# One inverse transform for all four heads: the full-height inverse of heads 0 and 1 replaced by the packed half-height one

## The chip, the cores and the metric

One core of one Trainium2 chip. The time is the device time of one execution in microseconds (us); where several executions are compared, it is the median. TensorE (PE, with its weight loads PEld), VectorE (DVE), ScalarE (ACT), GpSimd (POOL) and the DMA queue of SyncE (SP) work side by side, each strictly in its own order.

## The reference: what is computed

Two independent heads, concatenated along the last axis. Sequence 2048, width 512, float32.

```
A (FNet):  a = x @ Wd_re.T ; b = x @ Wd_im.T            # DFT over the width
           ya = Ws_re @ a - Ws_im @ b                    # DFT over the sequence, real part
B (S4D):   A = -exp(log_A_real) + 1j*A_imag ; dt = exp(log_dt)
           K[d,l] = 2*Re( sum_n C[d,n]*dt[d] * exp(A[d,n]*dt[d]*l) )      # 512 x 2048, 128 states
           y  = irfft( rfft(u, 4096) * rfft(K, 4096) )[:2048]            # causal convolution
           yb = y + u * D_skip
out = concat([ya, yb], -1)
```

## The kernel before, in words

**FNet** (class `Fnet`) is matmul work: 1920 matmuls of 128x128 by 128x512 (L312, tile `acc`). Each float32 operand is split into a rounded `hi` and a remainder `lo` (type fp32r), and three products hi*hi, hi*lo, lo*hi replace one. `split` (L147) does it: ScalarE copies `raw` into `hi` (L150), VectorE subtracts to get `lo` (L155). The first operand of all is `items[groups[0]][0]`, a tile `sT`; TensorE's first FNet matmul needs its `hi`. Some tiles take another way: GpSimd's DMA rounds and accumulates them (L248, L253). FNet has no deadline of its own: its matmuls fill TensorE between the steps of the other part.

**S4D** (class `Ssm`) runs as a chain of steps on four quarters of the width, h = 0 to 3 (`PART` = 128 columns each):

- VectorE builds exponential tables in 16 chunks (`tables1`, `tables2`; L531 to L648, tiles `t1`, `t2`, `prod`, `cs`, with seeds from ScalarE). For each chunk TensorE runs one `taps` block (L735), which needs both tables of the chunk. After every second chunk comes one block of `stage1_k` (L779): its result goes to DRAM as `xk`.
- u passes through `stage1_u` (L840): ScalarE and VectorE evacuate it (L851, L853, L855), it goes to DRAM as `xu`.
- For each quarter and q = 0 to 3, `product` loads `xu` and `xk`, runs the second stage of the forward transform (L975), multiplies on VectorE (L962 to L1000), and pairs of q go through the first stage of the inverse transform (`first_inverses`, L1009). The result is stored to DRAM as `zs` (L1047).
- The second stage of the inverse transform is run twice for each quarter (i = 0, 1). It loads `zs` transposed into a tile `zl`, does one TensorE block, is evacuated by ScalarE and stored to `out_yb`. There are two forms of it. `inverse` (L1122 on, quarters 0 and 1) uses the table `ib` with the whole height of 128 rows and two 128x64 tiles of the array side by side. `inverse2` (quarters 2 and 3, `HALVED` = 2) first adds and subtracts the two halves of the spectrum on VectorE (L1089, L1091), and then needs half of the rows: eight 64x32 tiles of the array side by side, with the table `ib2`. `ib2` is loaded over `ib` once all four calls of `inverse` are done (`load_ib2`).

**The order** of every engine's instructions is written out by hand: each coroutine yields the engine it wants next (`"pe"`, `"act"`, `"dve"`, `"dma"`, `"pool"`), and `Plan.run` steps them in the order of the list `ORDER`, some 2,700 numbers. `TURNS` is the order in which coroutines take the two PSUM tiles `f0` and `f1`. Buffers are counted with semaphores (`Sem`): `zls` for the tiles `zl`, `zbs` for the tiles `z` (`ZS` gives their number: 2 in the first set of buffers, 4 in the second).

The matmuls of the two forms, the old one and then the packed one:

```
for w in range(n // 2):            # inverse: 16 matmuls, K = 128, 64 columns
    for y in range(2):
        nc.tensor.matmul(ps[64 * y:64 * y + 64, ...], self.ib[:, n * i + 2 * w + y], z[:, 2 * w + y], ...,
                         tile_position=(0, 64 * y))
for o in range(0, c, 2):           # inverse2: 32 matmuls, K = 64, 32 columns
    for x in range(4):
        for y in range(2):
            nc.tensor.matmul(ps[32 * x:32 * x + 32, y, ...], self.ib2[r, c * i + w, x % 2], (t, z[:, 1])[x % 2][r, w], ...,
                             tile_position=(64 * y, 32 * x))
```

Of the kernel before, what the change touches and what calls it, by code (L numbers as in the profile page):

```python
# [26 lines left out]
def fft_constants():  # L27
# [24 lines left out]
    return [np.ascontiguousarray(a.astype(np.float32)) for a in (f1u, f1k, w2, ia, ib, ib2)]  # L52
# [70 lines left out]
class Fnet:  # L123
# [23 lines left out]
    def split(self, *tiles, n=None):  # L147
        yield "act"
        hi, _, src = tiles if n is None or n > 1 else self.first[self.turns["hi"].pop(0)]
        self.nc.scalar.activation(hi, src, AF.Copy)  # L150
        if not self.hi_ev.done:
            self.plan.set(self.hi_ev)
        yield "dve"
        hi, lo, src = tiles if n is None or n > 1 else self.first[self.turns["lo"].pop(0)]
        self.nc.vector.tensor_tensor(lo, src, hi.bitcast(F32), op=OP.subtract)  # L155
# [102 lines left out]
    def load(self, src, to, where, key, ev):  # L258
# [11 lines left out]
        yield from self.split(*to, raw)  # L270
# [76 lines left out]
class Ssm:  # L347


    def __init__(self, tc, ctx, plan, fnet, nd, ldt, dsk, uG, f1u, f1k, w2, ia, ib, ib2, out):  # L350
        self.tc, self.nc, self.plan, self.fnet = tc, tc.nc, plan, fnet
        self.nd, self.ldt, self.uG, self.ib2_in, self.out = nd, ldt, uG, ib2, out
# [8 lines left out]
        second, third = (("w2", w2), ("ib", ib)), (("ia", ia),)  # L361
# [8 lines left out]
        self.sets, self.set_ev, self.ib_ev, self.ib_left = {}, [Event(), Event()], Event(), 4  # L370
# [501 lines left out]
    def quarters(self):  # L872
# [11 lines left out]
        self.ib2_ev, self.loaded_ev = Event(), Event()  # L884
        self.pair, self.last, self.k_ev = [[] for _ in range(4)], [], Event()
        self.plan.spawn(self.load_ib2())
# [51 lines left out]
    def product(self, b, h, q, got, done):  # L938
# [65 lines left out]
        def run(got, o=0):  # L1004
            for c in range(2):
                for g in range(2):
                    for xx in range(4):
                        rows = slice(32 * xx, 32 * xx + 32)
                        nc.tensor.matmul(got[xx // 2][1][64 * g:64 * g + 64, xx % 2, o:o + 2 * PART], self.ia[rows, q // 2 if h >= HALVED else 0, c],  # L1009
                                         Y[c][rows, :, g], start=c == 0, stop=c == 1, tile_position=(32 * xx, 64 * g))  # L1010
# [42 lines left out]
    def inverses(self, h):  # L1053

        yield self.zs_ev[h][0]
        if h < 3:
            yield self.zs_ev[h][1]
        if h >= HALVED:
            yield self.set_ev[1]
        b = self.sets[int(h >= min(HALVED, 3))]  # L1060
        for i in range(2):
            yield b.zls
            self.plan.spawn((self.inverse2 if h >= HALVED else self.inverse)(b, h, i, 16))

    def load_ib2(self):
        yield self.ib_ev
        self.ib2 = self.ib[:, :16].rearrange("p n (a s) -> p n a s", a=2)
        yield "dma"
        self.nc.sync.dma_start(self.ib2, self.ib2_in)
        self.plan.set(self.ib2_ev)  # L1070

    def inverse2(self, b, h, i, n):
# [6 lines left out]
        for a in range(2):  # L1079
            yield self.zs_ev[h][a]  # L1080
            yield "act"
            nc.scalar.dma_start(z[64:, a], view[:, a, n * i + c:n * i + n])
            yield "dma"
            nc.sync.dma_start(z[:64, a], view[:, a, n * i:n * i + c])
        t = b.pool.tile([128, c, PART], F32, name="zsum", bufs=2 * b.n - 1)
        for w in range(0, c, 4):
            m = slice(w, w + 4)
            yield "dve"
            nc.vector.tensor_tensor(t[:, m], z[:, 0, m], z[:, 1, m], op=OP.add)  # L1089
            yield "dve"  # L1090
            nc.vector.tensor_tensor(z[:, 1, m], z[:, 0, m], z[:, 1, m], op=OP.subtract)  # L1091
# [13 lines left out]
        yield self.ib2_ev  # L1105
        got = yield from self.banks(len(two))
        yield "pe"
        for (_, _, run), (_, ps) in zip(two, got):
            run(ps)
        for (i, z, _), (k, ps) in zip(two, got):  # L1110
# [11 lines left out]
    def inverse(self, b, h, i, n):  # L1122

        nc = self.nc
        z = b.pool.tile([128, n, PART], F32, name="zl", bufs=b.n)
        yield "dma"
        for o in range(0, n, 8):
            nc.sync.dma_start(z[:, o:o + 8], self.zs[h].rearrange("s c l d -> (s c) l d")[:, n * i + o:n * i + o + 8])
        (k, ps), = yield from self.banks(1)
        yield "pe"  # L1130
        for w in range(n // 2):
            for y in range(2):
                nc.tensor.matmul(ps[64 * y:64 * y + 64, w // 4, PART * (w % 4):PART * (w % 4) + PART],  # L1133
                                 self.ib[:, n * i + 2 * w + y], z[:, 2 * w + y], start=True, stop=True,
                                 tile_position=(0, 64 * y))
        self.ib_left -= 1
        if not self.ib_left:
            self.plan.set(self.ib_ev)
        o = n * i // 2
        for w in range(0, n // 2, 4):  # L1140
            yield "act"
            nc.scalar.activation(z[:, w:w + 4], ps[:, w // 4].rearrange("p (w d) -> p w d", w=4), AF.Copy)
        self.give(k)
        yield "dma"
        nc.sync.dma_start(self.out[:, o:o + n // 2, PART * h:PART * h + PART], z[:, :n // 2])
        self.plan.put(b.zls)


ORDER = [
# [185 lines left out]
```

## Time and profile before

| what | value |
|---|---|
| median of 3 runs | 568.99 us (568.99 to 569.74) |
| the profiled execution | 569.5 us, its span 567.7 us |
| TensorE busy | 559.3 us, 99% of the span |
| VectorE busy | 505.6 us, 89% |
| ScalarE busy | 369.5 us, 65% |
| GpSimd busy | 50.3 us, 9% |
| moved by DMA | 135.53 MB, mean 239 GB/s |
| granted TensorE clock | 0.998 |

The span is measured from the first to the last event of the program in the profiled execution; its own time is 1.8 us longer. A line such as `L1133 PE MATMUL f<-zl,ib` names the source line, the engine, the operation, and the tiles written and read. "PE acc L312 x141" in the chain is a block of 141 FNet matmuls without a gap.

### The profile page before, as it was taken

The page shows a single profiled execution, that of the slowest core. Times are in us where ns is not written, and L with a number is a line of the kernel's source. Part 1 is how long each engine was busy: PE and PEld are TensorE (multiplying, and loading weights), DVE is VectorE, ACT ScalarE, POOL GpSimd, SP SyncE. Part 2 cuts the span into 40 slices and gives each one's busy share as a digit, 9 for nine tenths or more (in the row PEclk, how much of TensorE's full clock was granted, in tenths as well). Part 3 has the DMA queues.
Part 4 walks back from the last instruction along what each step waited for, and adds up shares of the span by engine and source line. Part 5 has one row for each costly group of instructions (what it writes and reads, how often), then busy time and mean ns, then how long its engine had stood idle before and what let it go on. Part 6 is the DMA issues. An engine that isn't in the chain of part 4 may idle for free.

```text
span 567.7 us, 15512 instructions
## 1 busy us (share of the span) xinstructions
PE 559.3 (99%) x6278; PEld 433.0 (76%) x6278; DVE 505.6 (89%) x846; ACT 369.5 (65%) x734; POOL 50.3 (9%) x74
## 2 busy tenths in 40 slices
PE   8999999999999999999999999999999999999995
PEld 6877776777878777777778778778787777777784
DVE  6979999999999999999999999999999998366640
ACT  5788736756686586868677776867876554355512
POOL 0001210021121112011111111111110000000000
PEclk9999999999999999999999999999999999999999
DMA  8989989998869858978799599679997899989776
GB/s 287 310 277 362 243 250 255 316 242 221 188 179 221 233 137 229 254 160 216 208 266 257 150 241 255 177 197 230 287 275 208 266 261 294 265 257 244 210 218 204
DMA packets 148855, 135.53 MB, mean 239 GB/s; under 512 B 47280, under 2 KB 107312, under 8 KB 148528
## 3 DMA queue, kind: packets, MB, share of 16 engines
q1 hardware_dynamic: 137776, 113.70, 67.2%
q0 software_dynamic: 10080, 18.35, 16.3%
q10 hardware_dynamic: 928, 2.49, 1.7%
q8 instruction: 49, 0.80, 0.6%
q14 instruction: 22, 0.18, 0.1%
HBM read 91.79 MB, written 42.73 MB: 237 GB/s over the span
## 4 chain that ended last, share of the span: by engine, by line
PE 98%; DMA 1%; ACT 0%; issue 0%
PE acc L312 79%; PE f L735 5%; PE f L975 5%; PE f L1009 3%; PE f L840 2%; PE f L779 1%; PE f L1133 1%; PE f L1098 1%; DMA raw<-in_sT 1%; ACT hi L150 0%; ACT y L321 0%; ACT zl L1113 0%
## 5 line engine op out<-in xcount | busy, mean ns | idle before, releaser
L312 PE MATMUL acc<-hi,x 128*128 128x512 f32 x1280 | 344.0, 395 | 0.3 <-ACT hi L150 0.3
L312 PEld LDWEIGHTS acc<-hi,x 128*128 128x128 f32 x1280 | 236.3, 188 | 67.5 <-issue 16.3
L312 PE MATMUL acc<-lo,x 128*128 128x512 f32 x640 | 189.6, 391 | 0.3 <-issue 0.3
L312 PEld LDWEIGHTS acc<-lo,x 128*128 128x128 f32 x640 | 119.7, 188 | 28.8 <-issue 3.3
L150 ACT ACTIVATE hi<-raw 128x512 fp32r<-128x512 f32 x125 | 77.2, 627 | 39.8 <-PE acc L312 19.3
L155 DVE TENSOR_TENSOR lo<-raw,hi 128x512 fp32r<-128x512 f32 x125 | 84.7, 686 | 20.0 <-ACT hi L150 15.6
L531 DVE TENSOR_TENSOR prod<-t,cs 128x128 f32<-128x128 f32 (+4 forms) x128 | 87.2, 695 | 1.1 <-ACT t L678 0.5
L547 ACT ACTIVATE square<-t 128x256 f32<-128x256 f32 (+1 forms) x64 | 36.8, 576 | 30.1 <-DVE t L540 25.8
L540 DVE TENSOR_TENSOR t<-prod 128x64 f32<-128x64 f32 (+4 forms) x128 | 53.0, 426 | 0.9
L253 POOL DMA_DIRECT2D lo<-in_sT x35 | 30.5, 872 | 246.6 <-ACT lo L251 134.0
L642 DVE TENSOR_TENSOR t<-t,cs 128x1024 f32<-128x1024 f32 x32 | 39.0, 1222 | 0.3
L648 DVE TENSOR_TENSOR t<-t,prod 128x1024 f32<-128x1024 f32 x32 | 39.1, 1221 | 0.1
L642 DVE TENSOR_TENSOR prod<-t,cs 128x1024 f32<-128x1024 f32 x32 | 39.0, 1220 | 0.0
L947 ACT ACTIVATE uk<-f 128x1024 f32<-128x1024 f32 x32 | 31.3, 1020 | 10.2 <-PE f L975 10.1
L326 ACT ACTIVATE y<-acc 128x512 f32<-128x512 f32 x47 | 26.7, 597 | 13.0 <-PE acc L312 13.0
L735 PEld LDWEIGHTS f<-t,t 128*32 128x32 f32 x2048 | 29.3, 110 | 5.5 <-issue 4.1
L248 POOL DMA_DIRECT2D hi<-in_sT x35 | 21.9, 626 | 127.2 <-PE acc L312 105.9
L735 PE MATMUL f<-t,t 128*32 128x64 f32 x2048 | 31.9, 220 | 0.0
L1037 ACT ACTIVATE z<-f 128x512 f32<-128x512 f32 x32 | 17.5, 603 | 19.8 <-PE f L1009 12.4
L251 ACT ACTIVATE lo<-hi 128x512 fp32r<-128x512 f32 x35 | 21.8, 624 | 10.6 <-DMA hi<-in_sT 10.3
L962 DVE TENSOR_TENSOR z<-uk 128x1024 f32<-128x1024 f32 (+1 forms) x20 | 20.1, 1009 | 7.4 <-ACT uk L947 7.3
L560 DVE TENSOR_TENSOR t<-square 128x128 f32<-128x128 f32 (+1 forms) x64 | 24.8, 388 | 1.1 <-ACT square L547 1.1
(107 smaller groups left out, 509.0 us busy)
## 6 DMA issues: line engine op xcount, KB each, us to landing
raw<-in_sT SPq DMA_DIRECT2D x92, 256.0 KB, 5.2
hi<-in_sT POOLq DMA_DIRECT2D x35, 256.0 KB, 5.7
lo<-in_sT POOLq DMA_DIRECT2D x35, 256.0 KB, 5.7
p<-y SPq DMA_DIRECT2D x32, 256.0 KB, 4.8
xk<-xk_sb SPq DMA_DIRECT2D x32, 256.0 KB, 4.7
zs<-z SPq DMA_DIRECT2D x32, 256.0 KB, 3.6
raw<-p SPq DMA_DIRECT2D x32, 256.0 KB, 5.1
xt<-xu SPq DMA_DIRECT2D x24, 256.0 KB, 5.1
```

The costliest lines, as they stand in the source:

```text
L150: self.nc.scalar.activation(hi, src, AF.Copy)
L155: self.nc.vector.tensor_tensor(lo, src, hi.bitcast(F32), op=OP.subtract)
L253: self.nc.gpsimd.dma_start(lo, src, accum_op=OP.add)
L312: self.nc.tensor.matmul(acc[d], still["hl".index(p[0])][:, 128 * d:128 * d + 128], m["hl".index(p[1])], start=i is items[0] and p == "hh", ...
L531: self.nc.vector.tensor_tensor(p.rearrange("p k d c m -> p k (d c) m"), src.rearrange("p d c l -> p (d c) l")[:, None, :, rows].to_broadca ...
L540: self.nc.vector.tensor_tensor(dst[:, :, :, rows], p[:, 0], p[:, 1, :, ::-1], op=OP.add)
L547: self.nc.scalar.activation(sq, t[:, :, :, m // 2:m], AF.Square)
L642: self.nc.vector.tensor_tensor(dst, t[:, :, :, rows], seed[:, k, :, :, None].to_broadcast([128, CHUNK, 2, n // 2 // CHUNK]), op=OP.mult)
L648: self.nc.vector.tensor_tensor(dst, dst, p[:, :, ::-1], op=OP.add)
L735: nc.tensor.matmul(ps[32 * j:32 * j + 32, i], t1[:, d, c], t2[:, d, c], start=c == 0, stop=c == 1, tile_position=(0, 32 * j))
L947: a.activation(uk[:, r].rearrange("p g c n d -> p g (c n d)"), p, AF.Copy)
L975: nc.tensor.matmul(got[r][1][32 * xx:32 * xx + 32, g, 256 * c:256 * c + 256], self.w2[rows, 2 * q + r, xx, 32 * c:32 * c + 32], xt[rows].r ...
```

## The change

`inverse` and `load_ib2` go; `inverse2` is now called `inverse` and serves all four quarters. For quarters 0 and 1 its loads are two DMAs on SP's queue, each to 64 partitions, and its sum `t` takes one of the tiles `z`, of which the first set of buffers now has 3. The first stage of the inverse transform uses two phase tables (`q // 2`) in all quarters. The table `ib` shrinks to `ib2` and is loaded once. The add and subtract on VectorE are one instruction each over 8x128 elements, where they were two over 4x128. The first `hi` of all is cast in two halves, by ScalarE and by VectorE. `ORDER` and `TURNS` are new lists. Line numbers shift: L150 to L152, L155 to L157, L312 to L314, L735 to L737, L779 to L781, L840 to L842, L853 to L855, L975 to L976, L1009 to L1010, L1098 to L1096, L1089 and L1091 to L1087 and L1089, L1113 to L1112.

```
     def split(self, *tiles, n=None, half=None):
         ...
-        self.nc.scalar.activation(hi, src, AF.Copy)
+        self.nc.scalar.activation(hi[:, :half], src[:, :half], AF.Copy)
+        if half:
+            self.nc.vector.tensor_copy(hi[:, half:], src[:, half:])
 ...
-        yield from self.split(*to, raw)
+        yield from self.split(*to, raw, half=256 if key == self.items[self.groups[0]][0] else None)
 ...
-                        ... self.ia[rows, q // 2 if h >= HALVED else 0, c],
+                        ... self.ia[rows, q // 2, c],
 ...
-            self.plan.spawn((self.inverse2 if h >= HALVED else self.inverse)(b, h, i, 16))
+            self.plan.spawn(self.inverse(b, h, i, 16))
 ...
+        if h < 2:
+            yield "dma"
+            for y in range(2):
+                nc.sync.dma_start(z[64 * y:64 * y + 64], view[:, :, n * i + c * y:n * i + c * y + c])
+            yield b.zbs
+            t = b.pool.tile([128, c, PART], F32, name="z", bufs=b.zn)
+        else:
+            ...
-        for w in range(0, c, 4):
-            m = slice(w, w + 4)
-            yield "dve"
-            nc.vector.tensor_tensor(t[:, m], z[:, 0, m], z[:, 1, m], op=OP.add)
-            yield "dve"
-            nc.vector.tensor_tensor(z[:, 1, m], z[:, 0, m], z[:, 1, m], op=OP.subtract)
+        yield "dve"
+        nc.vector.tensor_tensor(t, z[:, 0], z[:, 1], op=OP.add)
+        yield "dve"
+        nc.vector.tensor_tensor(z[:, 1], z[:, 0], z[:, 1], op=OP.subtract)
 ...
-HALVED = 2
-ZS = 2, 4
+ZS = 3, 4
 ORDER = [ ...
-    30, 20, 22, 21, 22, 30, 23, 24, 25, 20, 20, 22, 26, 21, 22, 1, 31, 23, 21, 31, 24, 23, 27, 31, 25, 24, 28, 31, 26,
 ...
-    60, 61, 68, 82, 4, 89, 99, 107, 113, 5, 6, 143, 144, 145, 13, 170, 13, 171, 13, 197, 172, 229, 13, 240, 230, 231,
+    60, 61, 68, 78, 88, 4, 94, 102, 109, 5, 6, 137, 138, 139, 13, 168, 13, 13, 193, 169, 13, 170, 222, 228, 243, 229,
```

What the new lists move is seen in the built programs, engine by engine. First VectorE ahead of its first operation on u (`zl<-f0`, L853 before); `lo` and `x12` to `x15` are FNet subtracts, `cs` and `seed` belong to the table seeds, `xk_sb` is the tile in which the parameters are worked out.

```order
L155 TENSOR_TENSOR lo_436<-raw_387,hi_435 128x512
L155 TENSOR_TENSOR lo_410<-raw_371,hi_409 128x512
L155 TENSOR_TENSOR x12_394<-uk_129,x12_394 128x512
L580 SCALAR_TENSOR_TENSOR seed_483<-seed_483 128x320
L155 TENSOR_TENSOR x13_401<-uk_129,x13_401 128x512
L853 TENSOR_TENSOR zl_430<-f0_447,zl_430 128x512
```

The same place of the changed kernel, VectorE up to its first operation on u (L855 now):

```order
L157 TENSOR_TENSOR x12_400<-uk_129,x12_400 128x512
L157 TENSOR_TENSOR x13_412<-uk_129,x13_412 128x512
L157 TENSOR_TENSOR lo_466<-raw_410,hi_465 128x512
L157 TENSOR_TENSOR lo_435<-raw_388,hi_434 128x512
L533 TENSOR_TENSOR prod_532<-t1_508,cs_477 128x128
L482 TENSOR_TENSOR xk_sb_126<-xk_sb_126,t1_166 128x384
L542 TENSOR_TENSOR t1_508<-prod_532 128x64
L157 TENSOR_TENSOR x15_438<-uk_129,x15_438 128x512
L582 SCALAR_TENSOR_TENSOR seed_490<-seed_490 128x320
L533 TENSOR_TENSOR prod2_555<-t2_123,cs_477 128x128
L855 TENSOR_TENSOR zl_440<-f0_454,zl_440 128x512
```

Parameter steps, table steps and FNet subtracts that came behind the first operation on u now stand ahead of it. Next VectorE in the middle of the changed kernel, where the first inverse of quarter 0 now has its add (`z<-zl`, L1087) and its subtract (L1089), in the middle of a chunk of the tables; `inverse` had no VectorE work there before.

```order
L533 TENSOR_TENSOR prod_3251<-t1_3197,cs_3104 128x256
L556 SCALAR_TENSOR_TENSOR t2_123<-t2_123 128x32x16
L644 TENSOR_TENSOR t2_123<-t2_123,cs_2712 128x64x16
L1087 TENSOR_TENSOR z_3218<-zl_3113 128x1024
L542 TENSOR_TENSOR t1_3197<-prod_3251 128x64x2
L1089 TENSOR_TENSOR zl_3113<-zl_3113 128x1024
L533 TENSOR_TENSOR prod_3310<-t1_3197,cs_3104 128x512
```

The table steps behind the two wait for them now, and they wait for the load of `zl_3113`. Last TensorE's end, before:

```order
L1098 MATMUL f0_7291<-zsum_7213,ib_113 32x128 x2
L1098 MATMUL f0_7291<-zl_7127,ib_113 32x128 x2
L312 MATMUL acc_7132<-hi_7186,x7_5653 128x512
L312 MATMUL acc_7132<-lo_7159,x6_5527 128x512
L312 MATMUL acc_7132<-lo_7187,x7_5653 128x512
```

TensorE's end in the changed kernel:

```order
L1096 MATMUL f0_7351<-zsum_7283,ib2_113 32x128 x2
L1096 MATMUL f0_7351<-zl_7193,ib2_113 32x128 x2
L314 MATMUL acc_7198<-hi_7227,x6_5566 128x512 x2
L314 MATMUL acc_7198<-hi_7247,x7_5599 128x512 x2
L314 MATMUL acc_7198<-lo_7228,x6_5566 128x512
L314 MATMUL acc_7198<-lo_7248,x7_5599 128x512
```

Six FNet matmuls follow the last inverse, where three did.

More of the change, by code (lines that the diff above doesn't have):

```diff
@@ L51, in fft_constants @@
     ib2 = ib[:64].reshape(64, 2, 2, 8, 32, 2).transpose(2, 0, 1, 3, 5, 4).reshape(128, 16, 2, 32)
-    return [np.ascontiguousarray(a.astype(np.float32)) for a in (f1u, f1k, w2, ia, ib, ib2)]
+    return [np.ascontiguousarray(a.astype(np.float32)) for a in (f1u, f1k, w2, ia, ib2)]
 class Sem:
@@ L145, in __init__, with split @@
         self.m, self.m_ev = {}, {i: Event() for g in self.groups for i in self.items[g]}
-    def split(self, *tiles, n=None):
+    def split(self, *tiles, n=None, half=None):
         yield "act"
         hi, _, src = tiles if n is None or n > 1 else self.first[self.turns["hi"].pop(0)]
-        self.nc.scalar.activation(hi, src, AF.Copy)
+        self.nc.scalar.activation(hi[:, :half], src[:, :half], AF.Copy)
+        if half:
+            self.nc.vector.tensor_copy(hi[:, half:], src[:, half:])
         if not self.hi_ev.done:
@@ L347, with __init__ @@
 class Ssm:
-    def __init__(self, tc, ctx, plan, fnet, nd, ldt, dsk, uG, f1u, f1k, w2, ia, ib, ib2, out):
+    def __init__(self, tc, ctx, plan, fnet, nd, ldt, dsk, uG, f1u, f1k, w2, ia, ib2, out):
         self.tc, self.nc, self.plan, self.fnet = tc, tc.nc, plan, fnet
-        self.nd, self.ldt, self.uG, self.ib2_in, self.out = nd, ldt, uG, ib2, out
+        self.nd, self.ldt, self.uG, self.out = nd, ldt, uG, out
         self.const = ctx.enter_context(tc.tile_pool(name="b_const", bufs=1))
@@ L360, in __init__ @@
         first = ("f1u", f1u), ("f1k", f1k), ("dskip", dsk)
-        second, third = (("w2", w2), ("ib", ib)), (("ia", ia),)
+        second, third = (("w2", w2), ("ib2", ib2)), (("ia", ia),)
         tiles = {n: self.const.tile([128, *a.shape[1:]], F32, name=n) for n, a in (*first[1:], *second, *third)}
@@ L369, in __init__ @@
         self.pars = Sem(1)
-        self.sets, self.set_ev, self.ib_ev, self.ib_left = {}, [Event(), Event()], Event(), 4
+        self.sets, self.set_ev = {}, [Event(), Event()]
         self.const_ev, self.const2_ev, self.const3_ev, self.xu_ev = Event(), Event(), Event(), Event()
@@ L883, in quarters @@
         self.plan.spawn(self.products())
-        self.ib2_ev, self.loaded_ev = Event(), Event()
+        self.loaded_ev = Event()
         self.pair, self.last, self.k_ev = [[] for _ in range(4)], [], Event()
-        self.plan.spawn(self.load_ib2())
         for h in range(4):
@@ L1008, in run @@
                         rows = slice(32 * xx, 32 * xx + 32)
-                        nc.tensor.matmul(got[xx // 2][1][64 * g:64 * g + 64, xx % 2, o:o + 2 * PART], self.ia[rows, q // 2 if h >= HALVED else 0, c],
+                        nc.tensor.matmul(got[xx // 2][1][64 * g:64 * g + 64, xx % 2, o:o + 2 * PART], self.ia[rows, q // 2, c],
                                          Y[c][rows, :, g], start=c == 0, stop=c == 1, tile_position=(32 * xx, 64 * g))
@@ L1053, in inverses, with inverse @@
     def inverses(self, h):
[L1055 to L1058, printed above, removed]
+        for a in range(1 + (h < 3)):
+            yield self.zs_ev[h][a]
+        if h > 1:
             yield self.set_ev[1]
-        b = self.sets[int(h >= min(HALVED, 3))]
+        b = self.sets[int(h > 1)]
         for i in range(2):
             yield b.zls
-            self.plan.spawn((self.inverse2 if h >= HALVED else self.inverse)(b, h, i, 16))
[L1065 to L1072, printed above, removed]
+            self.plan.spawn(self.inverse(b, h, i, 16))
+    def inverse(self, b, h, i, n):
         nc, c = self.nc, n // 2
@@ L1078, in inverse2 @@
             yield self.loaded_ev
[L1079 to L1082, printed above, removed]
+        if h < 2:
             yield "dma"
-            nc.sync.dma_start(z[:64, a], view[:, a, n * i:n * i + c])
-        t = b.pool.tile([128, c, PART], F32, name="zsum", bufs=2 * b.n - 1)
-        for w in range(0, c, 4):
-            m = slice(w, w + 4)
-            yield "dve"
-            nc.vector.tensor_tensor(t[:, m], z[:, 0, m], z[:, 1, m], op=OP.add)
-            yield "dve"
-            nc.vector.tensor_tensor(z[:, 1, m], z[:, 0, m], z[:, 1, m], op=OP.subtract)
+            for y in range(2):
[3 more added lines that the diff above has]
+        else:
+            for a in range(2):
+                yield self.zs_ev[h][a]
+                yield "act"
+                nc.scalar.dma_start(z[64:, a], view[:, a, n * i + c:n * i + n])
+                yield "dma"
+                nc.sync.dma_start(z[:64, a], view[:, a, n * i:n * i + c])
+            t = b.pool.tile([128, c, PART], F32, name="zsum", bufs=2 * b.n - 1)
+        yield "dve"
+        nc.vector.tensor_tensor(t, z[:, 0], z[:, 1], op=OP.add)
+        yield "dve"
+        nc.vector.tensor_tensor(z[:, 1], z[:, 0], z[:, 1], op=OP.subtract)
         def run(ps):
@@ L1104, in inverse2 @@
             return
-        yield self.ib2_ev
         got = yield from self.banks(len(two))
@@ L1109, in inverse2 @@
             run(ps)
+        if h < 2:
+            self.plan.put(b.zbs)
         for (i, z, _), (k, ps) in zip(two, got):
@@ L1120, in store_y @@
         self.plan.put(b.zls)
[L1122 to L1146, printed above, removed]
-ORDER = [
[104 rows of a table removed]
+ORDER = [
[104 rows of a table added]
 ]
 TURNS = [
[3 rows of a table removed]
[3 rows of a table added]
 ]
 CHUNK, FIRST = 32, 128
-HALVED = 2
-ZS = 2, 4
+ZS = 3, 4
 RAWS, DEPTH, STAGED = 5, 5, 4
@@ L1273, in program @@
         b = Ssm(tc, ctx, plan, a, i["nd"], i["ldt"], i["dsk"], i["uG"], i["f1u"], i["f1k"], i["w2"], i["ia"],
-                i["ib"], i["ib2"], o["yb"])
+                i["ib2"], o["yb"])
         tables = Event()
@@ L1291, in layout @@
     n = lambda a: np.asarray(a)
-    f1u, f1k, w2, ia, ib, ib2 = fft_constants()
+    f1u, f1k, w2, ia, ib2 = fft_constants()
     w = np.stack([n(A_dft_hid_re).T, n(A_dft_hid_im).T])
@@ L1306, in layout @@
         uG=u.reshape(32, 2, 16, 2, DM).transpose(3, 1, 0, 2, 4).reshape(128, 16, DM),
-        f1u=f1u, f1k=f1k, w2=w2, ia=ia, ib=ib, ib2=ib2)
+        f1u=f1u, f1k=f1k, w2=w2, ia=ia, ib2=ib2)
     return {k: np.ascontiguousarray(v) for k, v in arrays.items()}
@@ L1314, in assemble @@
 def assemble(ya, yb):
-    n = PART * HALVED
-    y1 = yb[:, :, :n].reshape(2, 64, 16, n).transpose(1, 2, 0, 3).reshape(SEQ, n)
-    y2 = yb[:, :, n:].reshape(2, 2, 32, 2, 2, 4, DM - n).transpose(2, 1, 3, 4, 5, 0, 6).reshape(SEQ, DM - n)
-    return np.concatenate([ya.T, y1, y2], axis=1)[None]
+    y = yb.reshape(2, 2, 32, 2, 2, 4, DM).transpose(2, 1, 3, 4, 5, 0, 6).reshape(SEQ, DM)
+    return np.concatenate([ya.T, y], axis=1)[None]
 def kernel(**inputs):
```

211 rows, old and new, of tables (ORDER, TURNS) are left out of this document.

## The prediction

> **What bounds the kernel now.** I read the page's busy times and its chain first, then the windows of one engine, then single places in the chain, the waits and the timeline.
>
> ```profile
> PE 559.3 (99%) x6278; PEld 433.0 (76%) x6278; DVE 505.6 (89%) x846; ACT 369.5 (65%) x734; POOL 50.3 (9%) x74
> PE 98%; DMA 1%; ACT 0%; issue 0%
> ```
>
> TensorE carries 98% of the chain that ended last, so a microsecond of matmul taken away is a microsecond gained, provided nothing else was about to be late. VectorE is the engine to check, and its share over the whole span hides where it works. By windows:
>
> ```profile
> core 0: us, DVE busy (x), PEclk, DMA share, GB/s
> 0.00:39.08 39.08, 30.45 (x66) 1.00 0.86 295
> 39.08:115.00 75.92, 73.75 (x125) 1.00 0.94 283
> 115.00:470.10 355.10, 349.96 (x581) 1.00 0.84 223
> ```
>
> Until 470 us VectorE is nearly full too: it idles 8.6 us up to 39.08, 2.2 up to 115, and 5.1 in the 355 us behind that. It builds the tables that the sixteen `taps` blocks (L735) on TensorE need; the last of these ends the stretch. Behind it VectorE has room. So there are two bounds side by side, and the change lowers one and loads the other.
>
> **The inverse on TensorE.** The chain in order of time (start, duration, what) has every block alone:
>
> ```profile
> 115.51 3.62 PE acc L312 x15
> 134.56 7.03 PE acc L312 x30
> 255.84 1.91 PE f L1009 x64
> 280.46 1.90 PE f L1133 x32
> 396.04 1.90 PE f L1133 x32
> 425.37 0.43 issue
> 471.22 1.92 PE f L735 x128
> 551.79 1.09 PE f L1098 x64
> 559.92 1.12 PE f L1098 x64
> ```
>
> (A block shows two records a matmul where both operands are plain fp32.) `inverse` (L1133) takes 1.90 us for 16 matmuls; `inverse2` (L1098) takes 1.09 and 1.12 for 32 matmuls of a quarter of the array each, with the same output. Four calls of the first kind become four of the second: 4 x (1.90 - 1.10) = -3.2. A block of FNet matmuls costs 0.21 fixed and 0.227 a matmul (from 15 and 30 of them), and the new order cuts the same 1920 into one block more: +0.2. TensorE in all: **-3.0**. The other TensorE groups keep number and shape. The 0.43 of "issue" lay inside one L1133 block, but nothing shows its cause: I take 0 of it and keep -0.4 for the low end. The two DMAs and two ScalarE evacuations a call remain in number and size; `ib` shrinks by half and its later reload goes, 1 MB of transfers less; I cost both at nothing, since TensorE waited for neither.
>
> **The first split.** ScalarE now does half of the first `hi`, VectorE the other.
>
> ```profile
> 4.15 0.63 ACT L150 ACTIVATE hi<-raw 128x512 fp32r<-128x512 f32 x1 [1.68 <-DMA raw<-in_sT]
> 4.81 0.69 DVE L155 TENSOR_TENSOR lo<-raw,hi 128x512 fp32r<-128x512 f32 x1 [0.35 <-ACT hi L150]
> 4.83 0.87 PE L312 MATMUL acc<-hi,x 128*128 128x512 f32 x2 [0.32 <-ACT hi L150]
> 5.55 0.50 PE L312 MATMUL acc<-lo,x 128*128 128x512 f32 x1
> ```
>
> The first two matmuls can start some 0.2 earlier, but the third waits for `lo`. That starts at 4.81 and cannot move up by more than its idle of 0.35, in which the new cast must be done as well. I take **-0.1**, between -0.3 and 0.
>
> **VectorE's new adds.** Each of the four calls now has an add and a subtract over 128x1024, which no earlier form of these calls had:
>
> ```profile
> 465.10 1.23 DVE L642 TENSOR_TENSOR t<-t,cs 128x1024 f32<-128x1024 f32 x1
> 466.24 1.22 DVE L642 TENSOR_TENSOR prod<-t,cs 128x1024 f32<-128x1024 f32 x1
> ```
>
> These start 1.14 apart, so 8 x 1.14 = 9.1 us. In the later calls (heads 2 and 3) four operations over 512 become two over 1024: about a microsecond less, in the tail, where VectorE has room. By the order of the changed kernel all eight adds stand ahead of the last table, with two FNet subtracts (0.62 each) and the cast (0.3) besides: VectorE's work up to there goes from 30.45 + 73.75 + 349.96 = 454.2 to 464.8. The last `taps` block stood at 471.22; in the new order it has 24 FNet matmuls and one block more ahead (+5.6), the four inverses are shorter (-3.2), the start -0.1: it is due at 473.5. So VectorE may idle 473.5 - 464.8 = 8.7 us up to there, where it idled 15.9. That is the question of this change. The same sum for the third to the fifteenth block gives rooms of that size, most of them 1 to 2 us larger, so they stand or fall together.
>
> What speaks for it is the order at the start. VectorE waited there for the seed (L600) and for the first bank of u (L853):
>
> ```profile
> DVE zl L853 <- ACT zl L851: 1.7, 1, 1.7
> DVE cs L600 <- ACT seed L591: 1.1, 1, 1.1
> 39.08 0.69 DVE L853 TENSOR_TENSOR zl<-f,zl 128x512 f32<-128x512 f32 x1 [1.69 <-ACT zl L851]
> ```
>
> Now 4.4 us of other work (two FNet subtracts, four parameter steps and three small table steps) stand ahead of the first u operation, and TensorE's u block comes three FNet matmuls later (+0.7). So VectorE has 34.8 us done when it can begin it at 39.7: idle 4.9 instead of 8.6. Behind that point, the waits that have a name are:
>
> ```profile
> DVE lo L155 <- ACT hi L150: 0.7, 1, 0.7
> DVE seed L580 <- ACT seed L578: 0.2, 1, 0.2
> DVE t L560 <- ACT square L547: 1.1, 1, 1.1
> DVE ks L751 <- ACT ks L741: 0.9, 1, 0.9
> DVE prod L531 <- ACT t L678: 0.5, 1, 0.5
> DVE xk_sb L764 <- ACT xk_sb L762: 0.4, 1, 0.4
> ```
>
> With a second L155 wait of 0.7 and one of 0.3 they come to 4.8 of the 7.3; the other 2.5 are steps between dependent operations and stay. If none of the named recurs, VectorE idles 4.9 + 2.5 = 7.4 and is in time; if all do, 12.2, and the last table is 3.5 late. Each hung on one neighbour in an order that is now another: I take half, 9.8, which makes TensorE wait **+1.1**, between 0 and +3.5.
>
> **The end.** The last result of all was the evacuated inverse, issued last:
>
> ```profile
> 561.27 0.63 PE L312 MATMUL acc<-lo,x 128*128 128x512 f32 x2
> 561.06 1.09 ACT L1113 ACTIVATE zl<-f 128x512 f32<-128x512 f32 x2 [0.21 <-PE f L1098]
> 563.05 0.43 SPq L1119 DMA_DIRECT2D out_yb<-zl  x1
> out_yb<-zl SPq DMA_DIRECT2D x8, 512.0 KB, 4.6
> 553.76 0.69 DVE L1091 TENSOR_TENSOR zl<-zl 128x512 f32<-128x512 f32 x1
> ```
>
> TensorE ended at 561.9, the span 5.8 later, at 563.05 + 4.6. Now six FNet matmuls (1.6 us) follow the last inverse instead of three. Its two evacuations (1.09) are over half a microsecond before TensorE ends, so that its 512 KB would land 4.2 behind that end: -1.6. The last transfers come closer together, though, and may delay each other; at the other bound nothing is gained. I take **-1.0**, nearer to the landing that the row shows. The merged adds give each last call a later first matmul, but VectorE was done 5.5 us before the last block (its last subtract ended at 554.4), and only about 1 of that goes.
>
> **Sum:** -3.0 - 0.1 + 1.1 - 1.0 = -3.0. The profiled execution took 569.5 (span 567.7 and 1.8 around it), so 566.5; the median of the runs is 568.99, 0.5 below it: **566.0 us**.
>
> **Rivals.** *VectorE is the bound and gives nothing back.* If its waits up to 39 us only change places, it idles 15.9 again, the last table is 7.2 late and so is everything behind it: 568.99 - 4.1 + 7.2 = 572.1, slower. It decides from a lateness of 4.1 on. For it: VectorE is 98% busy from 115 on. Against it: the two waits of 2.8 in the start have work in front of them now.
>
> *All named waits return.* 3.5 late: 568.99 - 4.1 + 3.5 = 568.4, no difference that can be told (a measurement of this kernel tells some 0.2%, 1.1 us).
>
> *The new adds wait for their data at VectorE's head.* An add that waits holds the tables behind it. The loads:
>
> ```profile
> 266.32 0.82 SPq L1128 DMA_DIRECT2D zl<-zs  x2
> zl<-zs SPq DMA_DIRECT2D x8, 512.0 KB, 5.9
> zl<-zs ACTq DMA_DIRECT2D x8, 256.0 KB, 6.2
> zl<-zs SPq DMA_DIRECT2D x8, 256.0 KB, 5.2
> ```
>
> In the order before, the load was issued 8.6 us after the L1009 block had ended (255.84 + 1.91) and landed some 6 us later: about 15 us. In the new order that block ends near 237.5, the load would land near 252.5, and VectorE reaches the first add near 253. That is the tight one; the other three have 5 us and more. If this load takes another 6 us, the time is 568.99 - 3.0 + 6 = 572, slower; it decides from 3 us on. The loads are now cut by partitions, 64 at a time, where they were cut by columns; the rows of 256 KB loads of 64 partitions show 5.2 and 6.2, nothing worse than the 512 KB ones. The Trainium skill ("DMA: Bandwidth & Descriptors", rules for kernel authors) advises against two transfers to disjoint partition halves, because they serialize on the same engines: by it the second half would land up to one transfer behind the first, which is this rival's case. The trace does not bear out a full doubling.
>
> *TensorE's time is not the limit.* Then the 3.2 turn into waiting and the time stays at 569. Against it: blocks of FNet matmuls follow each other with one slope and no gap. The Trainium skill ("Trainium Kernel Development and Optimization", best practices) says that matmul busy time is a poor measure of nearness to the roofline and that weight-load busy time is a good one; by that the 76% of PEld would leave room and this rival would hold. No wait in the chain supports it.
>
> **Chances.** Forecast with VectorE up to 2 us late: 0.70, own range 563.9 to 568.0. Late by 2 to 4.5: 0.16, near 568.4. VectorE the bound: 0.07. The adds' load: 0.04. Not the limit: 0.03. The low end is all gains at their best (-3.0 - 0.3 - 1.6 - 0.4 = -5.3, rounded up by what seldom meets), the high end takes in the second case: 563.9 to 569.2. Faster by over 0.2%: 0.73; within: 0.15; slower: 0.12.
>
> **What would show it.** Right: the four inverse blocks at about 1.1 us; VectorE idle about 5 us up to its first u operation and under 10 up to the last table; the last `taps` block near 474 to 475; the span ending some 5 us behind the last matmul. Wrong: VectorE waiting for `zl<-zs` before an L1087 add, or TensorE waiting for VectorE's tables ahead of `taps` blocks by more than 3 us in all; a gain in TensorE that shows up as idle TensorE; the inverse blocks costing more between FNet blocks in mid-kernel than in the tail.

## The result, and the profile after

| | median | runs | ratio to before, 95% interval |
|---|---|---|---|
| before | 569.62 us | 568.99 to 571.42 (6) | |
| changed | 565.91 us | 565.07 to 566.38 (6) | 0.9930 (0.9913 to 0.9947) |

Faster by 0.7%; the forecast was 566.0. The profiled execution of the changed kernel took 566.37 us, its span 564.6 (567.7 before). Its page, busy times and chain by engine:

```profile
PE 556.6 (99%) x6406; PEld 429.9 (76%) x6406; DVE 511.1 (91%) x847; ACT 369.6 (65%) x734; POOL 50.3 (9%) x74
PE 89%; DMA 4%; DVE 3%; ACT 2%; SPq 1%; issue 1%; DVEq 0%; ACTq 0%
```

TensorE's share of the chain fell from 98 to 89%, because early in the program the chain now leaves TensorE: up to 54.6 us it runs through loads, VectorE and ScalarE. The four inverses of heads 0 and 1, from the chain in order of time (start, duration, what):

```profile
258.26 1.09 PE f L1096 x64
282.06 1.09 PE f L1096 x64
369.31 1.09 PE f L1096 x64
406.77 1.09 PE f L1096 x64
```

Three of them stood at 1.90 before, the fourth, with the stop inside it, at 2.55. VectorE by windows, up to its first operation on u and up to the last table:

```profile
0.00:41.88 41.88, 34.52 (x76) 1.00 0.89 294
41.88:115.00 73.12, 72.53 (x122) 1.00 0.98 293
115.00:472.50 357.50, 355.61 (x586) 1.00 0.86 219
```

It idles 7.36 + 0.59 + 1.89 = 9.8 us, the sum forecast, but by luck: 7.4 of it (not 4.9) lie at the start, and 2.5 (not 4.9) behind it. The last table operation and the last `taps` block that needs it (start, duration):

```profile
470.70 1.22 DVE L650 TENSOR_TENSOR t<-t,prod 128x1024 f32<-128x1024 f32 x1
473.15 1.92 PE f L737 x128
```

The timeline shows a new wait at the start, what it led to, and the one add that waited; in brackets the idle time before an instruction and what ended it:

```profile
35.58 0.56 DVE L476 TENSOR_TENSOR xk_sb<-xk_sb,t 128x384 f32<-128x384 f32 x1 [1.66 <-DMA t<-dt_dram]
49.10 0.63 ACT L549 ACTIVATE square<-t 128x512 f32<-128x512 f32 x1 [1.88 <-DVE t L542]
49.75 1.28 ACT L589 ACT_TABLE_LOAD   x1
51.55 0.58 ACT L328 ACTIVATE y<-acc 128x512 f32<-128x512 f32 x1
53.63 0.72 PE L314 MATMUL acc<-hi,x 128*128 128x512 f32 x2 [0.16 <-ACT y L328]
254.87 1.23 DVE L1087 TENSOR_TENSOR z<-zl 128x1024 f32<-128x1024 f32 x1 [0.36 <-DMA zl<-zs]
```

One of the parameter steps moved to the front of VectorE's row waits 1.66 for a small load. VectorE stays late; a square at the head of ScalarE's row waits for it; behind the square stand a table load and the evacuations (L328) that give FNet its banks back, and the FNet block of 30 that TensorE begins at 50.78 takes 8.18 where 7.02 is usual. The tight first add waited 0.36.

The end: transfers of the last output, KB each and us from issue to landing, of before and then of the changed kernel:

```profile
out_ya<-y SPq DMA_DIRECT2D x1, 128.0 KB, 2.3
out_ya<-y ACTq DMA_DIRECT2D x1, 128.0 KB, 2.5
```

```profile
out_ya<-y SPq DMA_DIRECT2D x1, 128.0 KB, 4.4
out_ya<-y ACTq DMA_DIRECT2D x1, 128.0 KB, 3.9
```

TensorE's last piece in the chain of the changed kernel:

```profile
556.84 1.60 PE acc L314 x6
```

TensorE ends at 558.4 instead of 561.9 (-3.5), but by the landing records the last transfer lands 5.0 behind that end, where it was 4.7. In both kernels the span ends 1.1 behind the last landing. That is the span's -3.1.

### The profile page after: what moved, and what is told of

It is laid out like the page before. It is cut to its first block, busy times and chain, and to the rows that moved or that the text cites. A ratio compares the mean times of both kernels' runs of the same rounds, so it can differ in the third digit from the quotient of the medians.

```text
span 564.6 us, 15780 instructions
## 1 busy us (share of the span) xinstructions
PE 556.6 (99%) x6406; PEld 429.9 (76%) x6406; DVE 511.1 (91%) x847; ACT 369.6 (65%) x734; POOL 50.3 (9%) x74
## 4 chain that ended last, share of the span: by engine, by line
PE 89%; DMA 4%; DVE 3%; ACT 2%; SPq 1%; issue 1%; DVEq 0%; ACTq 0%
PE acc L314 72%; PE f L737 5%; PE f L976 5%; PE f L1010 3%; DMA raw<-in_sT 2%; PE f L1096 2%; PE f L781 1%; DMA uk<-in_x 1%; PE f L842 1%; DVE x L157 1%; DMA f1k<-in_f1k 1%; DVE lo L157 0%; DVE prod L533 0%; SPq L204 0%; ACT y L328 0%
## 5 line engine op out<-in xcount | busy, mean ns | idle before, releaser
L314 PE MATMUL acc<-hi,x 128*128 128x512 f32 x1280 | 346.4, 396 | 0.2 <-ACT y L328 0.2
L314 PEld LDWEIGHTS acc<-hi,x 128*128 128x128 f32 x1280 | 236.2, 188 | 69.5 <-issue 18.0
L314 PE MATMUL acc<-lo,x 128*128 128x512 f32 x640 | 188.8, 391 | 0.1
L314 PEld LDWEIGHTS acc<-lo,x 128*128 128x128 f32 x640 | 120.0, 188 | 27.3 <-issue 1.2
L157 DVE TENSOR_TENSOR lo<-raw,hi 128x512 fp32r<-128x512 f32 x125 | 84.6, 686 | 17.4 <-ACT hi L150 17.3
L150 ACT ACTIVATE hi<-raw 128x512 fp32r<-128x512 f32 (+1 forms) x125 | 76.9, 627 | 27.8 <-PE acc L314 12.7
L533 DVE TENSOR_TENSOR prod<-t,cs 128x512 f32<-128x512 f32 (+4 forms) x128 | 87.5, 695 | 0.9 <-ACT t L659 0.5
L542 DVE TENSOR_TENSOR t<-prod 128x256 f32<-128x256 f32 (+4 forms) x128 | 52.8, 425 | 0.6
L328 ACT ACTIVATE y<-acc 128x512 f32<-128x512 f32 x47 | 27.0, 597 | 24.3 <-PE acc L314 19.7
L650 DVE TENSOR_TENSOR t<-t,prod 128x1024 f32<-128x1024 f32 x32 | 39.0, 1220 | 0.0
L250 POOL DMA_DIRECT2D hi<-in_sT x35 | 19.8, 566 | 172.7 <-PE acc L314 152.9
L737 PEld LDWEIGHTS f<-t,t 128*32 128x32 f32 x2048 | 29.3, 110 | 5.7 <-issue 2.1
L737 PE MATMUL f<-t,t 128*32 128x64 f32 x2048 | 31.9, 220 | 0.0
L976 PE MATMUL f<-xt,w 64*32 64x256 f32 x768 | 23.5, 379 | 0.0
```

Of the source, the lines that this page charges most:

```text
L150: self.nc.scalar.activation(hi[:, :half], src[:, :half], AF.Copy)
L314: self.nc.tensor.matmul(acc[d], still["hl".index(p[0])][:, 128 * d:128 * d + 128], m["hl".index(p[1])], start=i is items[0] and p == "hh", ...
L533: self.nc.vector.tensor_tensor(p.rearrange("p k d c m -> p k (d c) m"), src.rearrange("p d c l -> p (d c) l")[:, None, :, rows].to_broadca ...
L542: self.nc.vector.tensor_tensor(dst[:, :, :, rows], p[:, 0], p[:, 1, :, ::-1], op=OP.add)
L650: self.nc.vector.tensor_tensor(dst, dst, p[:, :, ::-1], op=OP.add)
L737: nc.tensor.matmul(ps[32 * j:32 * j + 32, i], t1[:, d, c], t2[:, d, c], start=c == 0, stop=c == 1, tile_position=(0, 32 * j))
```

## The experiments

Every ratio is to runs of the kernel before on the same chip. Runs 1 to 4, 5 to 8 and 9 to 12 were made on three different chips, and of these the changed kernel itself ran only on that of 5 to 8. "The changed kernel" has 12 runs in all, 564.35 to 566.49, median 565.83.

**1. The packing in the old order.** From the kernel before: the constants, the phase tables and the new `inverse`, with its adds put where the loads had landed; all other steps as they were.

```
+        self.plan.step(("a", h, i), add())     # two steps on VectorE
 ORDER: the two steps inserted at 274.6 and 276.3, 307.9 and 308.6, 387.7 and 388.3, 420.0 and 421.7 us of the trace of before
```

> The kernel before with the packed inverse for all four heads (64 matmuls at 1.09 a block, the add and the subtract of 1.14 each ahead of them, the smaller constants), but with every other step where the kernel before has it; the eight adds stand where each load has landed. Theory: the packing alone takes 3.8 off TensorE, but the 9.1 us of adds then fall into a VectorE row whose 19 us of idle time lie in waits that the adds do not fill one for one, so tables come late for TensorE and half or more of the adds shows: 569 to 573, and gaps of TensorE ahead of taps blocks that the changed kernel does not have. Rival (the new order brings nothing, VectorE had room for the adds anyway): 565.5 to 566.5, no gap at the taps.

Measured: 579.26, ratio 1.0175 (1.0154 to 1.0196): 9.5 us slower than the 569.74 of before beside it. Both expectations missed; the direction was the theory's. What TensorE waited for (in all, times, longest):

```profile
PE f L1142 <- DVE zl L1134: 3.1, 2, 1.8
PE f L735 <- DVE t L648: 1.5, 1, 1.5
PE f L1142 <- issue: 1.3, 1, 1.3
PE f L975 <- issue: 0.9, 1, 0.9
PE f L1142 <- DVE zadd L1132: 0.7, 1, 0.7
```

From the start of each to the start of the block behind it, the four inverse blocks take 11.9 us in all instead of 4.4. They wait in the middle for their own subtract (3.1), since in the old order the matmuls come a few microseconds behind the load. A further 1.5 is the wait of the `taps` block behind the third for its table, and 1.3 a stop, with a granted clock of 0.50 from 431.85 to 438.68 us behind it. The waits before L975 (0.9, and another of 0.6) end when the two halves of `xt<-xk` have landed, at 291.37 and 292.89. So with the adds at these places the packing alone loses, and the new order is what makes room for them; other places in the old order were not tried.

**2. No adds.** 

```
-        nc.vector.tensor_tensor(t, z[:, 0], z[:, 1], op=OP.add)          # and the subtract; for h < 2
+        t = z[:, 0]
```

> The changed kernel without the eight adds and subtracts of heads 0 and 1: their matmuls read the two loaded halves themselves, so these two heads come out wrong. VectorE is freed of 9.1 us. Theory (no table is late for TensorE in the changed kernel, margins 0.5 to 11.5): no gain, 565.6 to 566.2. Rival (VectorE's row is the bound or shares it): TensorE is let go earlier at several places, 561 to 564.

Measured: 565.49 (564.65 to 566.74), ratio 0.9936 (0.9917 to 0.9954): no gain, as the theory said. VectorE has 8.2 us less to do between 115 and 472.5 and TensorE does not notice:

```profile
115.00:472.50 357.50, 347.46 (x578) 1.00 0.84 219
```

**3. More adds.**

```
+        for _ in range(1 + 2 * (h < 2)):
             nc.vector.tensor_tensor(t, z[:, 0], z[:, 1], op=OP.add)
```

> The changed kernel with the add of heads 0 and 1 carried out three times over instead of once, 8 x 1.14 = 9.1 us more on VectorE, nothing else. Theory: VectorE has idled 1.9 between 115 and 472.5 us and the tables' margins ahead of the taps are 0.5 to 2.8, so all beyond 2 to 3 us shows: 572 to 574, with TensorE waiting for tables. The prediction's own room (work up to the last table 464.8 against taps due at 473.5, 8.7 us): 566 to 567.

Measured: 574.40, ratio 1.0085 (1.0060 to 1.0110): 8.6 us of the 9.1 show, with 1.4 to either side. The theory's range was a little low. The longest of TensorE's waits:

```profile
PE f L1097 <- DVE zl L1090: 3.2, 3, 1.8
PE f L737 <- DVE t L650: 1.5, 2, 0.9
PE f L1097 <- DVE z L1088: 0.7, 1, 0.7
```

Only 1.5 of this is TensorE waiting for tables, as the theory had it; 3.9 are the packed blocks waiting for their own add and subtract, which the extra adds make later as well. With the second run, this puts the changed kernel near the edge: all of its adds are free, and little more would be at these places. (The margins quoted in this and two other expectations were read to the next-to-last table operation of a chunk. To the last, L650, they are 9.8 us at the first block, 0.2 to 5 at the others and 1.2 at the last.)

**4. The packed blocks run twice.**

```
-            run(ps)
+            for _ in range(1 + (h < 2)):
+                run(ps)
```

> The changed kernel with the four packed blocks of heads 0 and 1 run twice in a row, 4 x 64 matmuls more, about 4 x 0.98 = 3.9 us on TensorE alone. Theory (TensorE's own time is what ends the program, one for one): 569.5 to 570.2. Rival (the gain of the change came from elsewhere and TensorE's busy share is not the limit): 566 to 567.

Measured: 574.22 (572.24 to 574.68), ratio 1.0080 (1.0057 to 1.0103): 8.4 slower, twice the 3.9 expected for the matmuls. Neither expectation holds. The chain around the last doubled block:

```profile
408.19 1.92 PE f L737 x128
410.12 0.82 PE f L1096 x42
410.94 2.02 issue
412.95 1.14 PE f L1096 x41
```

Three doubled blocks take 1.96, 0.87 more than a single one; this one, right behind a `taps` block, takes 5.28, with a stop of 2.0 for which no operand, bank or load is to blame (the last section says what is). Behind the stop TensorE was granted half its clock for 3.4 us (window, its length, TensorE busy, PEclk, DMA share, GB/s):

```profile
413.35:416.76 3.41, 3.41 (x81) 0.50 0.54 162
```

Against the first profile of the changed kernel TensorE ends 8.2 later: 3.5 for the four doublings, 3.3 more in this block, 0.7 in the FNet block behind it, 0.6 in an FNet block with a shorter stop at 273.16, and 0.1 of small differences. So the added matmuls themselves show one for one, as the theory said, and the rest is stops and clock. The profiled execution has the wait at 51 us too (1.1).

**5 to 8.** Four kernels side by side: the changed kernel again, and three repairs.

> The changed kernel once more, as the measure for the three beside it: 565.3 to 566.5. In its profile the block of TensorE at 50.8 us is 1.1 longer than its matmuls (as in the changed kernel's first profile and in the runs with more adds and with the matmuls doubled) or not (as in the run without the adds, where VectorE happened to be earlier).

Measured: 565.52 (564.35 to 566.49), ratio 0.9928 (0.9912 to 0.9945). Its profiled execution, at 564.97, has no wait at 50 us (chain):

```profile
50.73 7.02 PE acc L314 x30
```

ScalarE's square did not wait (timeline; 49.10 in the first profile):

```profile
47.48 0.63 ACT L549 ACTIVATE square<-t 128x512 f32<-128x512 f32 x1
```

So the early wait is there in some executions only, and it goes with how late VectorE is by then: the load of `t` landed at 35.48 in the first and at 33.86 in this one. In ten profiled executions with L476 at its new place, it landed at 34.97 or later in six, all with TensorE's wait of 0.8 to 1.15, and at 34.01 or earlier in four, none with it. VectorE's first operation on u came at 41.3 or later in the six and at 40.3 or earlier in the four. The wait for `t` is not the only source of this: in runs 3 and 4 L476 waited only 0.18 and 0.36 for it, behind a wait of 1.9 for another load (`cs<-in_ldt`) at 11 us.

```
 ORDER: the steps of L476 and L478 behind the steps of x12, x13 and two lo
```

> The changed kernel with two steps of the seed parameters (L476, and L478 with ScalarE's L480 behind it) taken 10 places back in VectorE's row, behind two x splits and two lo steps whose data lie there already. In the profile of the changed kernel L476 waits 1.66 for the small load of t at the head of VectorE's row, ScalarE 2.19 for L478, and TensorE pays 1.5 at 50.8 us for evacuations that stand behind a late table step. Theory: the wait at 35 us goes, the first u op comes 1 to 2 us earlier than 41.8, TensorE's 1.15 at 50.8 goes: 0.7 to 1.5 faster than the changed kernel beside it. Rival (the wait at 50.8 is set by something else, or ScalarE's later L480 takes its place): 0 to 0.3.

Measured: 565.20 (564.72 to 565.67), ratio 0.9921 (0.9906 to 0.9936), 0.3 below the changed kernel beside it, which the intervals do not tell apart. The wait at 35 us is gone from its profile and the first u operation comes at 40.1, but the load landed at 34.75 there, where the wait might not have come anyway.

```
 ORDER: ScalarE's evacuation of d1 ahead of the square, that of d2 right behind it, d3's two places earlier
```

> The changed kernel with ScalarE's row alone changed at 48 us: the evacuations of banks d1 and d2 stand ahead of and right behind the square that waits for the late table step (not behind the table load and the seeds), d3's two places earlier. Theory (the banks were given back late because the square stood at the head of ScalarE's row): the 1.15 of TensorE at 50.8 goes; the seeds come 0.6 later, which eats into table margins of 0.5 and 0.8: 0.4 to 1.2 faster than the changed kernel beside it. Rival (TensorE waits there for the split tiles of the next group, not for banks): 0.

Measured: 565.67 (565.13 to 567.37), ratio 0.9937 (0.9920 to 0.9955): nothing to be told apart. The load landed at 34.01 in the profiled execution, so this profile cannot decide between banks and split tiles.

```
 ORDER, the end: head 3's second inverse block right behind its first, both stored, and only then the 12 matmuls of d2 and d3
```

> The changed kernel with its last 17 steps in another order: the inverse block of the last half of head 3 right behind that of its first half, both heads' halves evacuated and stored ahead of the last twelve matmuls of the y groups d2 and d3. Both 512 KB stores are then issued 1.5 to 2.5 us earlier, TensorE's work is the same. Theory (the last two halves of y, 128 KB each, land 3.9 to 4.4 us behind their issue instead of 2.3 because 1.25 MB of stores stand before them): they land in 2.5 to 3.3, 0.6 to 1.5 faster than the changed kernel beside it. Rival (the landing of these halves doesn't depend on what is in flight): 0 to 0.2.

Measured: 564.27 (563.72 to 564.83), ratio 0.9906 (0.9889 to 0.9923), 1.25 below the changed kernel beside it. Its last transfers:

```profile
out_ya<-y SPq DMA_DIRECT2D x1, 128.0 KB, 3.6
out_ya<-y ACTq DMA_DIRECT2D x1, 128.0 KB, 3.7
```

They land later than the theory's 2.5 to 3.3 but earlier than 4.4; from TensorE's end to the last landing it is 4.4 instead of 5.0 us. This 0.6 is shown by the profile; the rest of the 1.25 lies within the spread. By the view of DMA in time, some 290 GB/s or more flow in both kernels without a break while these stores run, so the tail is a matter of when they begin.

**9, 10. Half the matmuls (and half of their evacuations), with and without the adds.**

```
-            for o in range(0, c, 2):
+            for o in range(0, c if h > 1 else c // 2, 2):
```

> The changed kernel with half the matmuls of heads 0 and 1's inverse blocks (32 of 64 in each of four blocks, and half of each evacuation), so half of these heads' output is missing. TensorE has about 4 x 0.5 = 2.0 us less; the adds stay. The tables' margins ahead of the taps that follow are 0.8 to 4.3. Theory (TensorE's time ends the program one for one down to these margins): 1.3 to 2.1 faster than the changed kernel (565.5 to 565.9), 563.5 to 564.5. Rival (VectorE's row is already the second bound, and a saving of TensorE no longer shows): 0 to 0.5 faster.

> The same half of the matmuls, and the eight adds and subtracts of heads 0 and 1 left out as well, so that VectorE has 9.1 us less. Theory: the full 2.0 against the changed kernel, 563.5 to 563.9, and no more than 0.7 faster than with the adds. If VectorE shares the bound: 1 us or more faster than with the adds.

Measured: 565.87 (564.94 to 568.04), ratio 0.9934 (0.9916 to 0.9951), and 565.76 (564.95 to 565.99), ratio 0.9923 (0.9910 to 0.9936). Two microseconds of matmul less and no gain, the rival's time. But VectorE is not the reason, since the second has no adds. The chain of the first, at one of the four blocks and at two others, then of the second:

```profile
257.17 0.64 PE f L1096 x32
...
267.94 0.65 PE f L781 x7
268.59 0.72 issue
269.31 1.10 PE f L781 x25
...
375.99 1.03 PE f L781 x27
377.02 0.62 issue
```

```profile
299.55 1.00 PE f L976 x25
300.55 0.98 issue
301.53 1.48 PE f L976 x35
```

The blocks are shorter by 0.5 each, and stops as in run 4 have come up in blocks that nobody touched, which had none in the changed kernel. They take 1.3 and 1.0 of idle time, and the blocks grow by more than that: in the first run the L781 blocks take 11.0 in all where they took 8.4, in the second the L976 blocks 31.8 where they took 30.2.

**11. The first split on ScalarE alone.**

```
-        yield from self.split(*to, raw, half=256 if key == self.items[self.groups[0]][0] else None)
+        yield from self.split(*to, raw, half=None)
```

> The changed kernel with the first split on ScalarE alone, as in the kernel before. From the landing of the first raw tile to the first FNet matmul 0.71 instead of 0.50 (0.71 in the kernel before and in the old order, which both have it so). Theory: 0 to 0.3 slower than the changed kernel, too little to be told apart by time. Rival (the split is worth the 0.33 by which the first FNet matmul came earlier in the changed kernel's first profile): 0.3 to 0.5 slower.

Measured: 566.17 (565.18 to 567.44), ratio 0.9936 (0.9922 to 0.9951): not told apart from the changed kernel. From the landing of the first raw tile (4.05) to the first FNet matmul (4.76) it is 0.71, with the split 0.50.

**12. The two orders of 6 and 8 together.**

> The changed kernel with the two parameter steps later on VectorE and the other order of the last 17 steps together. Theory (the first keeps the early wait of TensorE from coming up in some executions, the second takes 0.6 to 0.9 off the end): 563.7 to 564.6, all executions under 565. Rival (the parameter steps do nothing): 563.7 to 564.9, as with the other tail alone.

Measured: 564.21 (564.11 to 564.47), ratio 0.9901 (0.9886 to 0.9916). It beats both kernels, 1.0% below the kernel before; and 1.6 us below the changed kernel's median of 12 runs, on other chips, of which one (564.35) is as low as these four. Its runs lie within 0.4 us of each other, those of the other tail alone within 1.1. That fits the theory that the moved steps take out the early wait, but four runs do not show it. VectorE does the moved steps without a wait:

```profile
34.68 1.29 DVE L157 TENSOR_TENSOR lo<-raw,hi 128x512 fp32r<-128x512 f32 x2
35.88 0.55 DVE L476 TENSOR_TENSOR xk_sb<-xk_sb,t 128x384 f32<-128x384 f32 x1
```

## Why the prediction was right, and where not

The total came out, in part by luck. Of its four terms one came out, one is too small to tell, and two failed in opposite directions; stops that went away and an early wait, neither of them in the sum, nearly cancel as well. Counted from the median before of all six runs, 569.62, the change is -3.7, where -3.0 was forecast from the 568.99 of the first three.

- *TensorE, -3.0.* Right: 4 x (1.90 - 1.09) = -3.2 and one FNet block more. Beside it, the stop in an L1133 block, which I took as 0, did not recur (that block took 2.55, -0.65), and two slow blocks of the execution before (L840 at 96.83, 1.78 instead of 1.04; L735 at 192.13, 2.31 instead of 1.92, with a stop at its end) were gone, against one L842 block (L840 before) that took 1.38 now: -0.8. Runs 4, 9 and 10 show that such stops come and go with the program, up to 2.0 each. This part of the gain was not the packing's.
- *The first split, -0.1.* Too small to tell. Counted from the landing of the first tile, the first matmul is 0.21 earlier and the third 0.08 later; in the trace's time the third moved from 5.55 to 5.51 because the tile landed 0.12 earlier. Run 11, without the split, is not told apart.
- *VectorE late, +1.1.* The step that failed is the work up to the last table: it ended at 471.92 with 462.1 us busy, not 464.8. With 9.8 idle it was 1.2 early, not 1.1 late, and no table held TensorE. Operations of 1.22 start 1.14 apart when they follow without a gap, so filling gaps makes the same work shorter by the profile's count; whether that is all of the 2.7 I did not settle. What I had as "room of 8.7" at the end was no room: of the 9.1 added in run 3, 0.5 was free, give or take 1.4.
- The forecast of 4.9 idle up to the first u operation failed too: it was 7.4, with 1.66 in the wait for `t` that I had not costed when a step on that load moved forward. It came back at another place than the tables, as 1.15 us of TensorE through ScalarE's row, and in some executions only.
- *The end, -1.0.* Failed: +0.3. I read the span's end as 563.05 + 4.6, but 4.6 is the median of eight stores; by the landing records this one took 3.6 and the span ended 1.1 behind it. And I counted on the landing of a transfer that has the queue to itself and named the crowding as the bound at which nothing is gained; with 1.25 MB of other stores still in flight the last ones took 3.9 and 4.4. Run 8 gets 0.6 back.

In the profiled pair: start -0.3, inverse blocks -3.8 (with the stop), slow blocks -0.8, one FNet block +0.2, waits in FNet blocks +1.2, the end +0.3: -3.2, against -3.1 measured. Of the signs named beforehand, the four blocks at 1.1 and the idle time under 10 came; the 5 up to the first u operation, the last `taps` block near 474 to 475 (it began at 473.15) and a span ending some 5 behind the last matmul (6.2) did not.

The rivals: *VectorE gives nothing back* and *all named waits return* did not come, though run 1 is the first of them in another form (the adds without the new order: +9.5). *The adds wait for their load*: 0.36 at the tight one, far from the 3 at which it decides. By the trace's landing records the four loads, now cut by partition halves, took 7.9 to 10.3 from the first issue to the second landing (8.8 at the tight one), where the column halves took 5.5 to 7.4, and the second half landed 2.0 to 2.4 behind the first, where it was 1.3 to 1.8. That is in the direction of the serializing that the Trainium skill warns of ("DMA: Bandwidth & Descriptors", rules for kernel authors), though no run separates it from the other traffic, and it is hidden here. *TensorE's time is not the limit*: neither it nor its opposite. Matmuls added cost double and matmuls removed brought nothing, since the stops moved; but the time followed TensorE's end in every profile. What the new order does with the old inverse was not run, so its own share of the gain stays open. The rule of the Trainium skill that I set beside this rival ("Trainium Kernel Development and Optimization", best practices: weight-load busy time is the better measure) would leave a quarter of the span free; run 4's added matmuls showed in full (3.5) and a stop on top, so here it does not hold.

## What to carry to other kernels

A change of shape and a change of order are two changes: price the new work against the order it will stand in, and ask of every step moved forward when its load lands. On an engine that is nearly full, what counts is the margin of each deadline, not the sum of idle time. Where an engine runs long stretches of very short instructions, a saving of a microsecond or two can vanish in, or come from, stops that have moved: take several variants before you credit it, and look at where the instruction packets land.

## What was not expected of the hardware

The stops without a releaser follow one pattern. The page lists a queue that moves only instructions:

```profile
q8 instruction: 50, 0.82, 0.6%
```

50 packets of 16 KB are 64 bytes for each of TensorE's 12,812 matmuls and weight loads. The kernel before has 12,556 of these and 49 packets, run 4 has 13,324 and 52, so this is taken to be TensorE's program. In the packet records, TensorE starts again soon after such a packet has ended: before, 192.81 to 194.44 and 424.35 to 425.80; run 1, 192.37 to 193.66, 401.09 to 402.38 and 430.97 to 432.41; run 4, 271.94 to 273.51 and 411.63 to 412.95; run 9, 268.01 to 269.31, 299.97 to 301.35 and 375.94 to 377.63; run 10, 300.26 to 301.53. That is 1.3 to 1.7 us eleven times; with 50 packets in 565 us a stop would end in that stretch by chance about once in 28.

Counting the instructions says more. Number all of TensorE's instructions in a trace (weight loads, matmuls and some hundred semaphore waits) from 0 in the order in which they start. The instruction on which it starts again has the number 256n + 193 in all eleven stops, and n is the number of packets that have ended by then: 9153 and 35 in the kernel before (425.80), 9409 and 36 in run 4 (412.95). In the fourteen traces no instruction with such a number starts less than 1.27 us behind the end of its packet. In the nine with the changed kernel's matmuls none starts less than 1.76 behind it, and none of the nine has such a stop. So in these stops TensorE waits for its own program, and they fall where the length of the program puts them: the 20th of these instructions stands in a `taps` block in the changed kernel (266.51), and in run 9, with 64 instructions less ahead of it, in an L781 block (269.31). The slow L840 block of the kernel before (96.83) has no packet near it; its cause stays open.

The Trainium skill ("Runtime: NRT & Kernel Launch", instruction fetch mechanics) says that instructions arrive in blocks of 16 KiB, 256 at a time, and that crossing a block is mostly hidden. The traces agree on the blocks, and on the hiding for most of the 50. Where 256 instructions are gone in 1.92 us, as in a `taps` block, a packet of 0.9 to 1.3 us with 1.3 behind it takes longer than the instructions it replaces. Runs 4, 9 and 10 moved the boundaries together with the number of matmuls; a run that moves them and nothing else was not made.

Behind two of the eleven stops (run 4 at 412.95, run 1 at 432.41) the granted clock fell to 0.50, for 3.4 and 6.8 us; why there and not behind the others stays open. The clock also spreads the start: in the fourteen profiled executions its record reaches 1.0 at 4.7 to 7.4 us, and until then FNet matmuls follow each other 0.43 apart instead of 0.23. By an estimate from these numbers that is up to 1.3 us between two executions, whatever the change.
